# Gated mix of linear and softmax attention: 88 row-maximum units in the front instead of 76, in single PSUM banks

## The chip, the cores and the metric

The kernel runs on one core of one Trainium2 chip. The metric is device time in microseconds (us), the median of the runs of the whole kernel. Engines are called as in the profile: PE is TensorE (matmul), PEld its weight load, DVE VectorE, ACT ScalarE, POOL GpSimd, SP SyncE (here only a queue for DMA).

## The reference

Two attention layers work on the same `x` (2048 x 448, 16 heads of 28). A is linear attention with a learned feature map, B is full softmax attention. A gate per token mixes their projected outputs.

```python
g = _sigmoid((x * gate_w).sum(-1, keepdims=True))
a = _A_ref(x, A_wqkv, A_w_phi, A_wo)
b = _B_ref(x, B_wqkv, B_wo)
return g * a + (1 - g) * b

# A
pq = einsum("bhsd,hdf->bhsf", q, w_phi);  pk = einsum("bhsd,hdf->bhsf", k, w_phi)
phi_q = concatenate([softmax(pq), softmax(-pq)], -1);  phi_k = (the same of pk)
kv = einsum("bhsf,bhsd->bhfd", phi_k, v);  z = phi_k summed over s
o = einsum("bhqf,bhfd->bhqd", phi_q, kv) / (einsum("bhqf,bhf->bhq", phi_q, z) + 1e-6)

# B
p = softmax(einsum("bhqd,bhkd->bhqk", q, k) * Dh ** -0.5)
o = einsum("bhqk,bhkd->bhqd", p, v)
```

Each of `o` is then laid out as 2048 x 448 and multiplied by its `wo`.

## The kernel before

**Stages.** The sequences of PE, DVE, ACT and POOL are written out by hand: each engine does its instructions in the order of the Python code. The order of the DMA issues on SP is the framework's. PE never goes on past a matmul that waits, so the place of every piece of work in the code is its place on PE.

1. *Projections of B's queries and keys* (`proj_qk`, matrices `pqk`), stored through SP to a scratch tensor `qkd`. The first projections take tiles from a list `later`.
2. *The front loop*, `for i in range(2 * NT + 11)` (L711 on; NT = 16 tiles of 128 tokens). `t = i` is a key tile and `q = i - NT` a query tile. For t below 16 it projects the keys (`pk`) and values (`pva`) of A and makes their features on ACT, DVE and POOL; for q from 0 it does the queries (`pq`, `pft`, `pn`), the output projection of A (`poa`, stored as `gad`), and, from q = NT + 2, the value projection of B (`value_b`, `pvb`) for tiles 0 to 7. `tok_major` (L120) makes each projection as a run of eleven matmul passes over high and low parts of input and weights, and calls a given function ahead of each pass; weights are loaded by part, split and folded (`split_part`, `fold`) on DVE and ACT. `pace` and `tick` (L703, L705) count the passes of `pk` of a pair of key tiles and call `mx_unit` at given counts.
3. *The last loop of the front* (`for t in range(8, NT)`, L888): `value_b` for tiles 8 to 15, seven with `mx_unit` between passes (77 passes), the last one with the scores of step 0.
4. *The late loop*: 256 steps. A step is one block of 128 keys by 512 queries for each of four heads: four score matmuls (`st`, L856), four exponentials on ACT (`p`, L872), and four value matmuls (`pv`, L1000), which the trace records as eight. The output of a group of heads is normalized and stored to `od` (`finish`, f1 to f4), and read back for the output projection at the end.

**Row maxima.** The exponentials need the maximum of each row of B's scores ahead. They are made for 16 groups `gq` (four groups of heads by four blocks of queries), each as 16 units of four heads by a block of 128 queries by 512 keys; 256 units in all. Each unit has four matmuls of 28 rows in 32-row tiles (one for each head). NF = 76 units are made in the front by `mx_unit` (L259), the other 180 in the late loop by `mx_visit`. The names GM and QM are NF split into whole groups and blocks: 76 = 4 x 16 + 4 x 3.

In `mx_unit` the four matmuls lie two by two in tiles of two banks: `pmb` and then `pmd` (L286). The relu of the whole `pmd` (128 x 1024) on ACT follows at L289, then two DVE operations (L291) which add `pmb` to one half each and take the maximum into a column of `part`. The front gives `pmb` and `pmd` tiles of one tag `mx` with two buffers; behind the second change of pools (`ps_s_.close()`, L882) `mx` has two buffers and `md` one. `mx_visit` makes four matmuls `pm` (L323), one relu (L327), and three DVE operations (L332, L335).

**Order in the late loop.** Steps 1 to 104 go as *doubles*: two steps' scores, two steps' values, one visit. Steps 105 to 232 go as *singles*, each with a visit. Steps from 233 on are doubles without visits, with output projections `pob` between. So V visits over 232 steps leave 2 x (232 - V) steps in doubles, since each double saves one visit (`first`, L1126).

**Step 0.** `scores(0, ...)` makes the scores of its four heads in two-bank tiles, with one exponential (L864) for two heads. The eight banks of the late loop are then taken over one by one (L916), in an order that follows which of the front's banks come free first.

**Loads of the units.** `pair_load` and `pair_query` issue the loads of a unit's keys (`kp`) and queries (`qp`), and POOL converts them. `take_acts`, `take_exps`, `take_subs`, `take_lows`, and `take_diffs` run work that was put aside earlier.

Of the kernel before, what the change touches and what calls it, by code (L numbers as in the profile page):

```python
# [8 lines left out]
F32 = mybir.dt.float32  # L9
# [8 lines left out]
P = 128  # L18
# [10 lines left out]
NU = NG * NQ * 16  # L29
NF = 76  # L30
LOWEST = -3.0e38
LAST = 232
OUTS = (200, 238, 246, 206)
PROJ = (235, 243, 251)
# [7 lines left out]
def gated_mix_kernel(ctx, tc, xT, wqkB, wvB, wvA, wkAT, wqAT, phi, woA, woB,  # L42
# [17 lines left out]

    psn = [3, 2]

# [5 lines left out]

    def ps_mx(nm, d):
        return ps.tile([P, 2, 512], F32, tag="md" if d and psn[1] == 3 else "mx", name=nm,  # L70
                       bufs=1 if d and psn[1] == 3 else 2)

# [187 lines left out]
    def mx_unit():  # L260

        u = mxs["u"]
        if u == NF:
            return
        mx_fin()
        take_diffs(2)
        mxs["u"] = u + 1
        gq, r = divmod(u, 16)
        g, qb = divmod(gq, NQ)
        if gq < GM:  # L270
            c, qt = divmod(r, 4)
            hp, b = divmod(c, 2)
            col = 64 * gq + 16 * b + 4 * qt + 2 * hp
            if r in (4, 9):
                pair_query(gq + 1, r // 9)
        else:
            c, qt = divmod(r, QM)
            hp, b = divmod(c, 2)
            col = 64 * gq + 4 * QM * b + 4 * qt + 2 * hp
            if r == 0:  # L280
                mx_query(gq)
        qc, kc = mxs[("qp", gq, hp)], mxs[("kp", g, c)]
        pb, pd = ps_mx(f"pmb{u}", False), ps_mx(f"pmd{u}", True)
        for j in range(4):
            js = slice(32 * j, 32 * j + DH)
            nc.tensor.matmul((pb if j < 2 else pd)[:, j % 2, :], qc[js, qt * P:(qt + 1) * P],  # L286
                             kc[js, :], start=True, stop=True, tile_position=(32 * j, 0))
        rl = rlp.tile([P, 2, 512], F32, tag="rl", name=f"rl{u}", bufs=2 if psn[1] == 3 else 1)
        nc.scalar.activation(rl, pd, AF.Relu)  # L289
        for i in range(2):  # L290
            nc.vector.tensor_tensor_reduce(rl[:, i, :], pb[:, i, :], rl[:, i, :], 1.0, LOWEST,  # L291
                                           ALU.add, ALU.max, part[:, col + i:col + i + 1])
        if gq < GM and qt == 3 and qb == NQ - 1:
            pair_load(g + 1, c)
        if gq == GM and qt == QM - 1:
            mx_load(g, c)
        if r == 15:
            mx_reduce(gq)
# [312 lines left out]
    def first_units():  # L611
# [7 lines left out]
        pqs = [ps_s(f"pqk0_{m}") for m in range(3)] + [ps_pv("pqk0_3")]  # L619
        pr = [ps_mx(f"pqk_{i}", False) for i in range(2)]  # L620
        later.extend((pr[0][:, 0, :], pr[1][:, 0, :], pr[0][:, 1, :]))
        for _ in range(8):
# [29 lines left out]
    for n in range(4, NP):  # L652
# [19 lines left out]
        if n in (16, 18):  # L672
            split_part(wvA_s, "wvA", 450, (n - 16) // 2)
            take_lows()
        if n in (10, 12, 14, 17):
            fold(wkA_s, "k", {10: 0, 12: 1, 14: 2, 17: 3}[n])
        if n == 10:
# [34 lines left out]
    for i in range(2 * NT + 11):  # L712
# [4 lines left out]
        if t < NT and t % 2 == 0:  # L717
            mx_unit()
            passes = (55 if t < NT - 4 else 44) + (4 if t >= 4 else 0)
            pace["n"], pace["at"] = 4 if t >= 4 else 0, [k * passes // 4 for k in (1, 2, 3)]  # L720
        if q in (0, 1):
# [44 lines left out]
        take_subs()  # L766
        if t == 1:
            pair_load(0, 3)
# [33 lines left out]
        if NT + 3 <= q < NT + 10:  # L802
            mx_unit()
        if q == NT + 2:
            bd_s.close()
            vb = [value_tile(0)]
        if 0 <= q - NT - 2 < 8:
            value_b(q - NT - 2)
        if y >= 5 and y % 2 and tb - 2 < 8:
# [40 lines left out]
    def scores(s, i, js=range(4)):  # L850
# [8 lines left out]
        if s == 0:  # L859
            p = at.tile([P, 2, 512], F32, name=f"p{s}_{i}")  # L860
            st = ps_mx(f"st{s}_{i}", i)
            for jl in range(2):
                score(2 * i + jl, st[:, jl, :])
            nc.scalar.activation(p, st, AF.Exp, scale=SCALE)  # L864
            pts.setdefault(s, []).extend([p[:, 0, :], p[:, 1, :]])
            return
# [13 lines left out]
    load_nm(0)  # L880
    ps_s_.close()
    ps = ps_s_.enter_context(tc.tile_pool(name="psv", bufs=1, space=PSUM, reuse_waits="tile"))  # L882
    psn[:] = 2, 3
    rlp = fr_s.enter_context(tc.tile_pool(name="rlp", bufs=1, reuse_waits="tile"))
# [30 lines left out]

    for i in (3, 4, 1, 2, 5, 6, 0, None):  # L916
        if i is None:
            ps2.tile([P, 512], F32, tag="pv", name="pv_first", bufs=1)
        else:
            bank(i, f"first{i}")  # L920
# [116 lines left out]
    def finish(gq, s):  # L1037
# [14 lines left out]
        def f4():  # L1052
            st["o"], = normalize4(late_p, st["n"], f"b{gq}", 1)
            if g < NG - 1:
                for j in range(4):
                    r = (4 * g + j) * DH
                    nc.sync.dma_start(o_d[r:r + DH, :, qb * 512:(qb + 1) * 512],
                                      f32(st["o"][32 * j:32 * j + DH]))

# [6 lines left out]
        late.setdefault(s + 8, []).append(lambda: acts.append(f4))  # L1066
        if g == NG - 1:
            for tl in range(4):
# [183 lines left out]
```

## Time and profile before

| | us |
|---|---|
| median of the runs shown | 1016.2 (1015.07 to 1016.46) |
| the profiled execution | 1016.56 |
| its span | 1014.8 |
| PE busy | 1004.8 |
| ACT busy | 818.1 |
| DVE busy | 647.5 |
| POOL busy | 250.9 |
| front, to the start of the first double | 363.75 |
| doubles with a visit (52) | 230.53 |
| singles with a visit (128) | 330.72 |
| the rest, to the end | 89.80 |

The granted TensorE clock is full in all of the 40 slices of the page. The stretches of the last four lines are cut where the chain of waits changes its pattern. A row of that chain gives the start, its length, and the instructions that it is made of; a row of the timeline the start, the time of one or several instructions, engine, line, operation, output and input. A row of the groups has busy time, mean nanoseconds of one, and the idle time of the engine ahead of them with what ended it. PE counts as busy while a matmul waits in its pipeline, so its busy share alone does not tell a stretch that PE limits from one in which it waits.

### The profile page before, as it was taken

What the parts mean: (1) busy time and instruction counts of PE and PEld (TensorE: products, weight loads), DVE (VectorE), ACT (ScalarE), POOL (GpSimd) and SP (SyncE); (2) the same over time, 40 slices, a digit from 0 to 9 for tenths busy, and PEclk for the clock granted to TensorE, in tenths of its full rate; (3) what the DMA queues carried; (4) which work ended last, traced back from release to release, by engine and by line L of the source; (5) the groups of instructions that cost most, each with busy time, mean ns of one, the idle gap of its engine ahead of it and who ended that gap; (6) DMA issues with size and microseconds to landing.
All of it is one profiled execution on the core that took longest, in us unless ns stands there. A gap on an engine that the chain in (4) does not pass through costs nothing.

```text
span 1014.8 us, 17693 instructions
## 1 busy us (share of the span) xinstructions
PE 1004.8 (99%) x6344; PEld 566.7 (56%) x6344; DVE 647.5 (64%) x1335; ACT 818.1 (81%) x1534; POOL 250.9 (25%) x218
## 2 busy tenths in 40 slices
PE   8999999999999999999999999999999999999998
PEld 7777877777777754444444443333333333335665
DVE  5467767898765535445444568888888788885112
ACT  5355655577765699999999999999999999997662
POOL 1225435578734820220110120110110101100010
PEclk9999999999999999999999999999999999999999
DMA  8874010113233671223542233342232247310441
GB/s 294 289 250 120 33 52 31 43 37 95 84 97 98 153 164 38 58 66 74 112 96 72 71 90 81 79 105 56 73 85 61 71 98 200 96 38 30 136 145 55
DMA packets 64570, 99.62 MB, mean 98 GB/s; under 512 B 18134, under 2 KB 24902, under 8 KB 64482
## 3 DMA queue, kind: packets, MB, share of 16 engines
q1 hardware_dynamic: 64482, 98.49, 35.8%
q8 instruction: 50, 0.82, 0.4%
q14 instruction: 38, 0.31, 0.1%
HBM read 70.29 MB, written 27.78 MB: 97 GB/s over the span
## 4 chain that ended last, share of the span: by engine, by line
PE 95%; DVE 3%; ACT 1%; DMA 1%; issue 0%; POOL 0%; DVEq 0%; ACTq 0%; POOLq 0%
PE st L856 28%; PE pv L1000 24%; PE pm L323 8%; PE pqk L110 5%; PE poa L110 4%; PE pk L128 4%; PE pva L128 4%; PE pmb L286 3%; PE pob L110 3%; PE pq L110 2%; PE pvb L110 2%; PE pvb L128 2%; PE pn L538 1%; PE pqk L640 1%; PE pft L526 1%; DVE featq L453 1%
## 5 line engine op out<-in xcount | busy, mean ns | idle before, releaser
L872 ACT ACTIVATE p<-st 128x512 f32<-128x512 f32 x1020 | 525.1, 639 | 26.4 <-PE st L856 26.4
L335 DVE TENSOR_REDUCE part<-pm 128x1 f32<-128x512 f32 x405 | 258.8, 685 | 178.7 <-PE pm L323 178.7
L856 PE MATMUL st<-qst,kst 128*128 128x512 f32 x1024 | 299.5, 422 | 0.1
L1000 PE MATMUL pv<-p,vb 128*32 128x512 f32 x2048 | 259.7, 601 | 0.0
L856 PEld LDWEIGHTS st<-qst,kst 128*128 128x128 f32 x1024 | 171.0, 187 | 101.6 <-ACT p L872 39.3
L425 POOL TENSOR_TENSOR oUb<-oUb,rsb 128x512 f32<-128x512 f32 x15 | 19.3, 1289 | 492.4 <-DMA rsb<-rdb 360.1
L291 DVE CUSTOM_DVE_ANT_0 rl<-pmb,rl 128x512 f32<-128x512 f32 x152 | 98.3, 684 | 57.0 <-ACT rl L289 57.0
L327 ACT ACTIVATE rl<-pm 128x512 f32<-128x512 f32 x180 | 111.5, 620 | 10.4 <-PE pm L323 10.0
L323 PEld LDWEIGHTS pm<-kc,qc 28*128 28x128 f32 x720 | 34.4, 181 | 150.9 <-ACT p L872 102.3
L289 ACT ACTIVATE rl<-pmd 128x1024 f32<-128x1024 f32 x76 | 78.1, 1028 | 38.2 <-PE pmd L286 31.0
L1000 PEld LDWEIGHTS pv<-p,vb 128*32 128x32 f32 x2048 | 50.5, 108 | 96.0 <-issue 93.6
L332 DVE CUSTOM_DVE_ANT_0 rl<-pm,rl 128x512 f32<-128x512 f32 x135 | 92.0, 681 | 0.0
L323 PE MATMUL pm<-kc,qc 28*128 28x512 f32 x720 | 91.2, 495 | 0.0
L110 PE MATMUL pqk<-XH,wB 128*128 128x512 f32 x192 | 59.6, 397 | 1.7 <-DVE ev L578 1.7
L577 ACT CAST ev<-pqk 128x512 fp32r<-128x512 f32 x28 | 15.9, 588 | 36.7 <-PE pqk L110 32.0
L110 PE MATMUL poa<-woA_s,oTa 128*128 128x448 f32 x192 | 43.4, 375 | 0.0
L110 PEld LDWEIGHTS pqk<-XH,wB 128*128 128x128 f32 x192 | 35.3, 188 | 10.6 <-DVE ev L578 2.2
L1011 DVE SCALAR_TENSOR_TENSOR acc<-pob,gate,acc 128x448 f32<-128x448 f32 x12 | 8.2, 684 | 50.8 <-PE pob L110 50.8
L128 PE MATMUL pk<-wkA_s,XH 128*128 128x448 f32 x128 | 39.5, 382 | 0.0
L286 PE MATMUL pmd<-kp,qp 28*128 28x512 f32 x152 | 38.0, 496 | 0.8 <-DVE part L291 0.8
L110 PEld LDWEIGHTS poa<-woA_s,oTa 128*128 128x128 f32 x192 | 34.9, 188 | 6.2 <-issue 3.2
L128 PE MATMUL pva<-wvA_s,XH 128*128 128x450 f32 x128 | 37.8, 371 | 0.0
(155 smaller groups left out, 1196.1 us busy)
## 6 DMA issues: line engine op xcount, KB each, us to landing
qkd<-ev SPq DMA_DIRECT2D x28, 512.0 KB
qst<-qkd SPq DMA_DIRECT2D x64, 224.0 KB
kst<-qkd SPq DMA_DIRECT2D x64, 224.0 KB
od<-oTb SPq DMA_DIRECT2D x48, 112.0 KB
rsa<-rda SPq DMA_DIRECT2D x8, 512.0 KB
rsb<-rdb SPq DMA_DIRECT2D x15, 256.0 KB
gad<-ga SPq DMA_DIRECT2D x16, 224.0 KB
acc<-gad SPq DMA_DIRECT2D x4, 896.0 KB
```

What stands on the lines that cost most here:

```text
L110: nc.tensor.matmul(dst, l, r, start=i == 0, stop=i == len(todo) - 1)
L128: nc.tensor.matmul(dst[:, :n], l, r, start=i == 0, stop=i == len(todo) - 1, skip_group_check=True)
L286: nc.tensor.matmul((pb if j < 2 else pd)[:, j % 2, :], qc[js, qt * P:(qt + 1) * P], kc[js, :], start=True, stop=True, tile_position=(32 * ...
L289: nc.scalar.activation(rl, pd, AF.Relu)
L291: nc.vector.tensor_tensor_reduce(rl[:, i, :], pb[:, i, :], rl[:, i, :], 1.0, LOWEST, ALU.add, ALU.max, part[:, col + i:col + i + 1])
L323: nc.tensor.matmul(pm[j], mxs[("qc", gq)][js, qt * P:(qt + 1) * P], mxs[("kc", g, kb)][js, :], start=True, stop=True, tile_position=(32 * ...
L327: nc.scalar.activation(rl, pm[kb], AF.Relu if kb < 3 else AF.Copy)
L332: nc.vector.tensor_tensor_reduce(r, pm[j], r, 1.0, LOWEST, ALU.add, ALU.max, part[:, col + j:col + j + 1])
L335: nc.vector.tensor_reduce(part[:, col + j:col + j + 1], pm[j], AX.X, ALU.max)
L856: nc.tensor.matmul(st, kst_of[(g, kt // 4)][:, j, (kt % 4) * P:(kt % 4 + 1) * P], qst_of[gq][:, j, :], start=True, stop=True)
L872: nc.scalar.activation(p, sts[j], AF.Exp, scale=SCALE)
L1000: nc.tensor.matmul(pv[32 * j:32 * j + 32, :], vb[kt // 8][:, kt % 8, 4 * g + j, :], pt[j], start=kt == 0, stop=kt == NT - 1, tile_position ...
```

## The change

- NF goes from 76 to 88: twelve units more in the front (5 x 16 + 4 x 2), twelve visits fewer in the late loop (168). `first` becomes 128.
- A unit uses single banks: four tiles of tag `mx` with four buffers (six after the change of pools), in the order d0, d1, b0, b1. Two relus of 128 x 512, each followed by the DVE operation that reads it. The tile `rl` has two buffers of 512.
- `pace` asks for five units to a pair of key tiles for t below NT - 4 and four after.
- The change of pools moves from before the last loop to q = NT + 6 in the front loop. Behind it `s` has two banks and `mx` six.
- `value_b` of q = NT + 6 to NT + 9 has a unit behind its pass 4.
- The folds of the key weights go from n = 10, 12, 14, 17 to 11, 13, 15, 18; `pair_load(0, 3)` from t = 1 to t = 0.
- The three tiles `later` are single banks.
- A head's stores go from f4 at step s + 8 to f5 at s + 13; the fourth entry of OUTS, a step at which the output's data is read back, from 206 to 210.
- Step 0 makes one exponential for each head; the order of the first banks in the late loop follows the new tiles.

```diff
@@ -27,10 +27,10 @@
 SCALE = DH ** -0.5
 EPS = 1e-6
 NU = NG * NQ * 16
-NF = 76
+NF = 88
 LOWEST = -3.0e38
 LAST = 232
-OUTS = (200, 238, 246, 206)
+OUTS = (200, 238, 246, 210)
 PROJ = (235, 243, 251)
 
 
@@ -58,7 +58,7 @@
     ps = ps_s_.enter_context(tc.tile_pool(name="ps", bufs=1, space=PSUM, reuse_waits="tile"))
     dr = ctx.enter_context(tc.tile_pool(name="dr", bufs=1, space=DRAM))
 
-    psn = [3, 2]
+    psn = [3, 4, 2]
 
     def ps_s(nm):
         return ps.tile([P, 512], F32, tag="s", name=nm, bufs=psn[0])
@@ -66,9 +66,8 @@
     def ps_pv(nm):
         return ps.tile([P, 512], F32, tag="pv", name=nm, bufs=1)
 
-    def ps_mx(nm, d):
-        return ps.tile([P, 2, 512], F32, tag="md" if d and psn[1] == 3 else "mx", name=nm,
-                       bufs=1 if d and psn[1] == 3 else 2)
+    def ps_mx(nm):
+        return ps.tile([P, 512], F32, tag="mx", name=nm, bufs=psn[1])
 
 
     def scratch(nm, shape):
@@ -280,16 +279,18 @@
             if r == 0:
                 mx_query(gq)
         qc, kc = mxs[("qp", gq, hp)], mxs[("kp", g, c)]
-        pb, pd = ps_mx(f"pmb{u}", False), ps_mx(f"pmd{u}", True)
+
+        pm = [ps_mx(f"pm{'ddbb'[j]}{u}_{j % 2}") for j in range(4)]
         for j in range(4):
-            js = slice(32 * j, 32 * j + DH)
-            nc.tensor.matmul((pb if j < 2 else pd)[:, j % 2, :], qc[js, qt * P:(qt + 1) * P],
-                             kc[js, :], start=True, stop=True, tile_position=(32 * j, 0))
-        rl = rlp.tile([P, 2, 512], F32, tag="rl", name=f"rl{u}", bufs=2 if psn[1] == 3 else 1)
-        nc.scalar.activation(rl, pd, AF.Relu)
+            i = (j + 2) % 4
+            js = slice(32 * i, 32 * i + DH)
+            nc.tensor.matmul(pm[j], qc[js, qt * P:(qt + 1) * P], kc[js, :], start=True, stop=True,
+                             tile_position=(32 * i, 0))
         for i in range(2):
-            nc.vector.tensor_tensor_reduce(rl[:, i, :], pb[:, i, :], rl[:, i, :], 1.0, LOWEST,
-                                           ALU.add, ALU.max, part[:, col + i:col + i + 1])
+            rl = rlp.tile([P, 512], F32, tag="rl", name=f"rl{u}_{i}", bufs=psn[2])
+            nc.scalar.activation(rl, pm[i], AF.Relu)
+            nc.vector.tensor_tensor_reduce(rl, pm[2 + i], rl, 1.0, LOWEST, ALU.add, ALU.max,
+                                           part[:, col + i:col + i + 1])
         if gq < GM and qt == 3 and qb == NQ - 1:
             pair_load(g + 1, c)
         if gq == GM and qt == QM - 1:
@@ -617,8 +618,7 @@
             nc.sync.dma_start(raw[b][:, 1, :], xT[:, b, :512])
         x_loads(1)
         pqs = [ps_s(f"pqk0_{m}") for m in range(3)] + [ps_pv("pqk0_3")]
-        pr = [ps_mx(f"pqk_{i}", False) for i in range(2)]
-        later.extend((pr[0][:, 0, :], pr[1][:, 0, :], pr[0][:, 1, :]))
+        later.extend(ps_mx(f"pqk_{i}") for i in range(3))
         for _ in range(8):
             nc.tensor.matmul(pqs[3][:, :P], ident, ident, start=True, stop=True)
         for b in range(4):
@@ -672,8 +672,8 @@
         if n in (16, 18):
             split_part(wvA_s, "wvA", 450, (n - 16) // 2)
             take_lows()
-        if n in (10, 12, 14, 17):
-            fold(wkA_s, "k", {10: 0, 12: 1, 14: 2, 17: 3}[n])
+        if n in (11, 13, 15, 18):
+            fold(wkA_s, "k", {11: 0, 13: 1, 15: 2, 18: 3}[n])
         if n == 10:
             pair_query(0, 0)
             pair_load(0, 0)
@@ -716,8 +716,9 @@
         take_acts()
         if t < NT and t % 2 == 0:
             mx_unit()
-            passes = (55 if t < NT - 4 else 44) + (4 if t >= 4 else 0)
-            pace["n"], pace["at"] = 4 if t >= 4 else 0, [k * passes // 4 for k in (1, 2, 3)]
+            passes, n = (55, 5) if t < NT - 4 else (44, 4)
+            passes += 4 if t >= 4 else 0
+            pace["n"], pace["at"] = 4 if t >= 4 else 0, [k * passes // n for k in range(1, n)]
         if q in (0, 1):
             take_exps()
 
@@ -764,7 +765,7 @@
         if 2 <= q - 1 < NT:
             fq[q - 1] = features2(fq[q - 1], f"q{q - 1}")
         take_subs()
-        if t == 1:
+        if t == 0:
             pair_load(0, 3)
         if y >= 8 and y % 2 == 0 and tb - 4 < 8:
             num[tb - 4] = normalize3(*num[tb - 4], 2)
@@ -801,11 +802,15 @@
             turn(y - 2)
         if NT + 3 <= q < NT + 10:
             mx_unit()
+        if q == NT + 6:
+            ps_s_.close()
+            ps = ps_s_.enter_context(tc.tile_pool(name="psv", bufs=1, space=PSUM, reuse_waits="tile"))
+            psn[:2] = 2, 6
         if q == NT + 2:
             bd_s.close()
             vb = [value_tile(0)]
         if 0 <= q - NT - 2 < 8:
-            value_b(q - NT - 2)
+            value_b(q - NT - 2, lambda i: mx_unit() if i == 4 and q >= NT + 6 else None)
         if y >= 5 and y % 2 and tb - 2 < 8:
             num[tb - 2] = normalize2(ta, *num[tb - 2], f"a{tb - 2}", 2, True)
     ta_s.close()
@@ -857,12 +862,11 @@
                              qst_of[gq][:, j, :], start=True, stop=True)
 
         if s == 0:
-            p = at.tile([P, 2, 512], F32, name=f"p{s}_{i}")
-            st = ps_mx(f"st{s}_{i}", i)
-            for jl in range(2):
-                score(2 * i + jl, st[:, jl, :])
-            nc.scalar.activation(p, st, AF.Exp, scale=SCALE)
-            pts.setdefault(s, []).extend([p[:, 0, :], p[:, 1, :]])
+            for j in (2 * i, 2 * i + 1):
+                p, st = at.tile([P, 512], F32, name=f"p{s}_{j}"), ps_mx(f"st{s}_{j}")
+                score(j, st)
+                nc.scalar.activation(p, st, AF.Exp, scale=SCALE)
+                pts.setdefault(s, []).append(p)
             return
         sts = {j: bank(b, f"st{s}_{j}") for j, b in zip(js, i)}
         for j in js:
@@ -878,9 +882,6 @@
     stg = at
     load_q(0)
     load_nm(0)
-    ps_s_.close()
-    ps = ps_s_.enter_context(tc.tile_pool(name="psv", bufs=1, space=PSUM, reuse_waits="tile"))
-    psn[:] = 2, 3
     rlp = fr_s.enter_context(tc.tile_pool(name="rlp", bufs=1, reuse_waits="tile"))
     mx_unit()
     rest = NF - mxs["u"]
@@ -913,7 +914,7 @@
         return ps2.tile([P, 512], F32, tag=f"g{i}", name=nm, bufs=1)
 
 
-    for i in (3, 4, 1, 2, 5, 6, 0, None):
+    for i in (0, None, 2, 3, 1, 6, 5, 4):
         if i is None:
             ps2.tile([P, 512], F32, tag="pv", name="pv_first", bufs=1)
         else:
@@ -1051,11 +1052,12 @@
 
         def f4():
             st["o"], = normalize4(late_p, st["n"], f"b{gq}", 1)
-            if g < NG - 1:
-                for j in range(4):
-                    r = (4 * g + j) * DH
-                    nc.sync.dma_start(o_d[r:r + DH, :, qb * 512:(qb + 1) * 512],
-                                      f32(st["o"][32 * j:32 * j + DH]))
+
+        def f5():
+            for j in range(4):
+                r = (4 * g + j) * DH
+                nc.sync.dma_start(o_d[r:r + DH, :, qb * 512:(qb + 1) * 512],
+                                  f32(st["o"][32 * j:32 * j + DH]))
 
         if last:
             finish_last(gq)
@@ -1064,7 +1066,9 @@
         late.setdefault(s + 3, []).append(f2)
         late.setdefault(s + 7, []).append(f3)
         late.setdefault(s + 8, []).append(lambda: acts.append(f4))
-        if g == NG - 1:
+        if g < NG - 1:
+            late.setdefault(s + 13, []).append(f5)
+        else:
             for tl in range(4):
                 mids[PROJ[qb] + tl] = lambda tl=tl: project(qb, st["o"], tl)
 
```

## The prediction, written before the changed kernel was run

> **What bounds the kernel now.** I read the chain of waits of the page first, then the busy time by stretch with its boundaries at the changes of structure, then the chain inside each stretch.
>
> ```profile
> PE 95%; DVE 3%; ACT 1%; DMA 1%; issue 0%; POOL 0%; DVEq 0%; ACTq 0%; POOLq 0%
> ```
>
> TensorE ends 95% of the chain, but "busy TensorE" means two things, as the stretches show (us; busy time and count of PE, PEld, DVE, ACT, POOL; granted clock, DMA share, GB/s):
>
> ```profile
> 340.00:363.75 23.75, 23.70 (x124) 16.78 (x124) 13.85 (x44) 16.17 (x22) 21.30 (x13) 1.00 0.86 180
> 363.75:594.28 230.53, 230.53 (x1452) 105.52 (x1452) 109.41 (x222) 230.37 (x466) 25.62 (x26) 1.00 0.36 82
> 594.28:925.00 330.72, 330.72 (x2050) 126.90 (x2049) 270.41 (x544) 320.51 (x641) 31.80 (x29) 1.00 0.35 84
> ```
>
> The last loop of the front (first row) is a TensorE stretch: 23.70 of 23.75, ACT 16.17, DVE 13.85. 363.75 to 594.28 holds the 52 doubles (steps 1 to 104, one visit for two steps); 594.28 to 925.00 holds the 128 singles (a visit for each step). ACT is busy 230.37 of 230.53 in the doubles and 320.51 of 330.72 in the singles: there TensorE's time is waiting, and ACT sets the pace. 466 instructions in 230.53 are 0.495 us each, nine to a double (eight exponentials, one relu), which is also the distance of the starts below, although one lasts 0.6:
>
> ```profile
> 594.30 0.60 ACT L327 ACTIVATE rl<-pm 128x512 f32<-128x512 f32 x1
> 594.80 2.06 ACT L872 ACTIVATE p<-st 128x512 f32<-128x512 f32 x4
> ```
>
> The same stretches as the chain shows them, one double and then a single and the start of the next (start us, us, what):
>
> ```profile
> 367.03 2.17 PE st L856 x8
> 369.19 1.85 PE pv L1000 x16
> 371.05 0.44 PE pm L323 x4
> ...
> 596.89 1.40 PE st L856 x5
> 598.29 0.99 PE pv L1000 x8
> 599.29 0.43 PE pm L323 x2
> 599.72 0.90 PE st L856 x3
> 600.62 0.99 PE pv L1000 x8
> ```
>
> **The late loop gains 8.8.** Twelve more units in the front are twelve visits fewer, 168 for 180, so 24 steps go from singles to doubles (64 doubles, 104 singles). A double takes 230.53/52 = 4.433, 2.217 per step; a single 330.72/128 = 2.584. 24 x (2.584 - 2.217) = 8.8. The other end: if only the twelve relus went from a full ACT and the idle time of the singles stayed, 12 x 0.495 = 5.9. I take 8.8, since each mode keeps its rate over its whole stretch.
>
> **The front's price is 7.4.** A unit in the front and what it does to the run of projection passes it cuts:
>
> ```profile
> 247.37 2.46 PE poa L110 x12
> ...
> 308.20 0.42 PE pmb L286 x2
> 308.62 0.16 PE pmd L286 x2
> 308.78 2.65 PE poa L110 x12
> ...
> 338.32 1.63 PE pvb L128 x7
> 339.95 0.42 PE pmb L286 x2
> ```
>
> Twelve passes behind other passes take 2.46, 0.205 each; behind a unit 2.65, 0.19 more. Seven in the last loop: 7 x 0.205 = 1.44 against 1.63, again 0.19. So a unit costs its 0.42 to 0.43 and a restart of 0.19: 0.62. Each of the twelve new units cuts a run: in the built order four lie in the pairs of key tiles t = 4 to 10 (five units now), four within value tiles at q = 22 to 25, four in the last loop (15 units over its 77 passes, before 11). 12 x 0.62 = 7.4. Lower bound, where a restart falls on one that is there already: 12 x 0.43 = 5.2. I take 7.4. The fifth unit of pairs t = 0 and 2 can't come: its place is pass 44 and the two tiles count passes 0 to 43.
>
> **Waits that go: 2.7.** The row of 308.62 is one of seven between 295 and 333 in which the d matmuls wait about 0.16 for the bank that the unit before still reads: 1.1. Three more stand at t = 12 to 15, two of them shown:
>
> ```profile
> 168.59 0.50 PE pmd L286 x2
> ...
> 174.84 0.60 DVE rl L291
> ...
> 175.50 0.50 PE pmd L286 x2
> ...
> 182.13 0.49 PE pmd L286 x2
> ```
>
> Their d matmuls, which should add 0.01 after the b, add 0.49 to 0.50 each at 168.59 and 182.13, and at 175.50 the 0.50 ends a wait for the two reductions of the unit before. That is 0.48 for each of the outer two and about 0.6 for the middle one, 1.6 in all. With single banks a first half is free as soon as its own relu or reduction ends, and d needs only the unit before the last.
>
> **Waits that come: 3.6.** What a unit's banks wait for follows from these (ACT and DVE in the timeline; the unit starts at 317.55 and at 339.95):
>
> ```profile
> 317.66 0.63 ACT L553 ACTIVATE ga<-poa,gate 128x448 f32<-128x448 f32 x1 [1.57 <-PE poa L110]
> 318.19 1.02 ACT L289 ACTIVATE rl<-pmd 128x1024 f32<-128x1024 f32 x1
> ...
> 340.48 1.03 ACT L289 ACTIVATE rl<-pmd 128x1024 f32<-128x1024 f32 x1 [0.32 <-PE pmd L286]
> 341.55 0.69 DVE L291 CUSTOM_DVE_ANT_0 rl<-pmb,rl 128x512 f32<-128x512 f32 x1 [0.81 <-ACT rl L289]
> 342.17 0.08 DVE L291 DVE_READ_ACCUMULATOR2_ANT part<- 128x1 f32 x1
> ```
>
> The relu starts 0.53 behind the unit's start. Two half relus of 0.60 start 0.50 apart (the late rows), so the second ends at 0.53 + 0.50 + 0.60 = 1.63. With six banks in the order d0 d1 b0 b1, b0 and b1 of a unit take the banks of the relus of the unit just before; d0 and d1 those of the reductions two units before.
> - Last loop: 15 units in 77 passes, so 0.43 + 0.19 + 5.1 x 0.205 = 1.67 from unit to unit (2.06 now: 1.63 + 0.43). The second relu ends at 1.63, which leaves 0.04 for handing over the bank; I take that a unit is late by as much, 15 x 0.04 = 0.6.
> - q = 23 to 25: the unit within the value tile follows 0.43 + 0.19 + 4 x 0.205 = 1.44 after another whose relus stand behind the copy ga (317.66): the first relu starts at 318.19 - 317.55 = 0.64, the second ends at 1.74 and a handover later: 3 x 0.33 = 1.0.
> - The pools are now changed at q = 22: the unit behind the change takes its b banks from the reductions of the unit 1.44 before, done at 0.53 + 0.60 + 0.62 (distance of two reductions) + 0.69 + 0.08 = 2.5, with handovers 2.6: 1.2. The wait at the old place of the change (before the last loop) gives back 0.2.
> - Front: the unit behind the fold that moves to n = 18 finds DVE and ACT with the weights, and five units to a pair leave slack of 0 to 0.4 in the rest: 0.3 + 0.3, and about 0.4 of the 1.6 above stays at t = 12 to 15.
> Sum 0.6 + 1.0 + 1.2 - 0.2 + 0.6 + 0.4 = 3.6. From below: if none comes, 0; from above 3.6 + 3.9 (next part).
>
> **Moved at no cost.** The head's four stores go from step s + 8 to s + 13. They are issued on SP, behind no step of the chain (DMA has 1% of it in all); what would be late is the next use of the tile, 16 steps after the last, so 3 steps stand between. The first pair load comes one tile earlier; its conversion is POOL's, which has 0% of the chain, and the folds that move one pass on meet idle time of DVE in most tiles (if not hidden, the 0.3 above). The three `later` banks of the first projections end the sharing of a tile, for which one projection waits today:
>
> ```profile
> L110 PE MATMUL pqk<-XH,wB 128*128 128x512 f32 x192 | 59.6, 397 | 1.7 <-DVE ev L578 1.7
> ```
>
> The loads of the input set what follows, and they do not move, so I count 0 of this 1.7; it is the upper gain. In step 0 four exponentials of 512 stand for two of 1024: about 0.1 more, in the handover.
>
> **Sum.** -8.8 + 7.4 - 2.7 + 3.6 = -0.5, on the profiled execution's 1016.56 (span 1014.8 and 1.76 around it): 1016.1. It lies 0.36 above the median 1016.2, so 1015.7 against the median.
>
> **The rivals.**
> *Free rotation (faster).* The new short waits do not come: all 3.6 go, 1015.7 - 3.6 = 1012.1; half of them, 1013.9. For it: my latencies of 1.63 and 1.74 stand so close to the intervals that 0.05 decides. Against: in the present rows a d that waits for a unit's reductions does show its 0.16 seven times. The Trainium skill, Perfetto Trace Analysis, section on matmul optimizations, says that independent matmul groups should rotate through different banks so that the evacuation of one overlaps the next group's matmuls; six single banks do it more fully, and by that rule this rival is the one. The trace bears it out only where the interval is above the evacuation's length: at 2.06 in the last loop the row of ACT shows its 0.32 of idle time and no lateness.
>
> *The evacuation becomes the bound (slower).* In the last loop ACT and DVE, not TensorE, set the distance of units. Per unit ACT has two relus and 7/15 of a copy:
>
> ```profile
> L700 ACT COPY vb<-pvb 128x448 f32<-128x448 f32 x16 | 8.5, 530 | 12.2 <-PE pvb L110 9.4 <-POOL vb L693 1.7 <-PE pvb L128 0.9
> ```
>
> That is 0.50 + 0.60 + 0.25 = 1.35 of 1.67; DVE by the row of 340 to 363.75 has 13.85/11 = 1.26. Both fit on average, but the order is fixed by hand: a copy of 0.53 between a relu and its matmul moves the chain to about 1.97. Then 15 x 0.3 = 4.5 in place of 0.6, +3.9: 1015.7 + 3.9 = 1019.6. It decides from the point at which the second relu ends later than 1.67 behind its unit. Against: today the row of 340.48 shows ACT idle before each relu. The Trainium skill, TensorEngine Tiling (Array Packing), section on the PSUM bottleneck, says that tiling speeds up TensorE but not the evacuation, and advises vectorizing access over tiles in one bank; the change does the reverse, one relu of 1.03 becomes two of 0.60. By that rule this rival is what happens.
>
> *Late loads (slower).* The late loop's first key chunk now has less time between its last load and its first visit:
>
> ```profile
>   DMA kc<-qkd: 20.0, 1
>   POOL kc L197: 0.8, 1
> ```
>
> POOL waited 20.0 for it, and one visit waited 0.8 for POOL. Some 2 us of lead go, as the last loop starts its loads in proportion to its length; two visits at 1 to 1.5 each: +2.5, 1018.2.
>
> *It doesn't do what it says.* The five to two tiles do not come in two pairs, which the sum has. If the four others also failed, they would go to the last loop: 19 in 77 passes, 1.45 apart, each 0.2 late: +3.8, 1019.5.
>
> **Chances and range.** Forecast, a sum between 1014.2 and 1018.2: 0.42. Free rotation 0.29, evacuation 0.20, late loads 0.06, not as it says 0.03. A measurement of this kernel tells about 0.2%, 2.0 us, from no change (the three runs span 1.4): faster is below 1014.2, slower above 1018.2. Faster 0.29, same 0.42, slower 0.29. The range reaches from the full free rotation, 1012.1, to the evacuation's 1019.6: 1012.2 to 1019.6; the forecast's own is 1014.2 to 1018.2.
>
> **What would show it.** The doubles with visits should last 64 x 4.433 = 283.7 and the singles 104 x 2.584 = 268.7, 552.4 together for 561.25 now. The start of the doubles should move from 363.75 by +8.3. In the last loop units 1.67 to 1.70 apart agree, 1.9 or more is the evacuation. At q = 22 one wait of a b matmul for DVE near 1.2, none larger. The d matmuls at 295 to 333 should lose their 0.16. Wrong would be a wait for DMA at the first visits, singles slower than 2.6, or a front more than 10 longer.

## The result and the profile after

| | before | after |
|---|---|---|
| median of 7 runs, us | 1015.77 (1014.87 to 1016.46) | 1018.49 (1015.58 to 1020.85) |
| ratio to before, 95% interval | | 1.0023 (1.0013 to 1.0034) |
| profiled execution, us | 1016.56 | 1018.49 |
| its span, us | 1014.8 | 1016.7 |
| mean granted TensorE clock of the profiled execution | 1.000 | 0.998 |

The changed kernel is slower by 0.23%, some 2.3 us, where no measurable change was forecast (-0.5). The late loop did gain, the front lost more than that, and TensorE's clock was cut for 3.4 us near the start of the profiled run. Six of the seven runs have a mean granted clock of 0.997 or 0.998; the seventh, at 1.000, is the one of 1015.58.

First the page's share of the chain of waits after, to be held against the 95% of before:

```profile
PE 92%; DVE 4%; DMA 2%; ACT 1%; issue 0%; SPq 0%; DVEq 0%; ACTq 0%
```

TensorE's share fell by three points, but that is not 30 us of new waits: all waits in the view of TensorE's waits add up to 7.0 us, against 6.1 before. The chain is followed back through the wait near 33 us, and ahead of it now runs over the loads, stores and copies of the start, where before it ran mostly over TensorE; but for the waits below, TensorE was busy there in both. The view of TensorE's waits names those that differ most (waited for: us in total, times, longest), before and then after:

```profile
PE pqk L110 <- DVE ev L578: 1.7, 1, 1.7
PE pwk L393 <- issue: 1.4, 1, 1.4
```

```profile
PE pqk L109 <- DVE ev L579: 3.8, 1, 3.8
PE pv L1001 <- DVE oUb L405: 0.9, 1, 0.9
PE pmb L287 <- ACT rl L291: 0.7, 1, 0.7
```

The two waits of before near 22 and 36 us have become one of 3.8; two new ones stand in the late loop (pv) and among the first units (pmb). The stretches after (columns as in the prediction), around the wait of 3.8 and then the doubles, the singles and the end:

```profile
33.00:36.00 3.00, 0.04 (x1) 0.00 (x0) 0.65 (x1) 1.72 (x3) 0.60 (x1) 1.00 1.05 405
36.00:39.00 3.00, 2.18 (x5) 1.81 (x6) 1.93 (x4) 0.78 (x2) 2.00 (x9) 0.61 0.57 212
39.00:42.00 3.00, 3.00 (x16) 2.55 (x16) 0.23 (x1) 0.58 (x1) 0.00 (x0) 0.82 0.99 269
372.58:657.49 284.91, 284.91 (x1793) 130.98 (x1792) 134.94 (x274) 284.75 (x577) 33.35 (x33) 1.00 0.37 82
657.49:927.20 269.71, 268.79 (x1665) 103.19 (x1665) 219.89 (x442) 260.45 (x521) 24.15 (x22) 1.00 0.36 85
927.20:1016.70 89.50, 85.99 (x477) 55.35 (x476) 17.58 (x32) 48.18 (x95) 5.08 (x5) 1.00 0.31 101
```

TensorE does nothing from 33 to 36, and behind that the clock is 0.61 and 0.82 over three us each: (0.39 + 0.18) x 3 / 0.5 = 3.4 us at half clock, a loss of 1.7. A double takes 284.91/64 = 4.452, a single 269.71/104 = 2.593; both rates are those of before within 0.02, so each of the two modes works as it did (the seam between them comes below).

Where the time went shows when the same matmul is looked up in both traces (the n-th of its input and output, counted from 0), and 0.62 is taken off for each unit that one trace has ahead of it more. "Rest" is what is left, and grows where the changed kernel loses:

| matmul | before, us | after, us | units ahead | rest |
|---|---|---|---|---|
| projection of B, 112th of XH | 46.53 | 47.70 | 0 / 0 | +1.16 |
| first `pk` (key tile 0) | 67.46 | 69.57 | 5 / 5 | +2.11 |
| `pk` of key tile 12 | 160.12 | 165.62 | 29 / 33 | +3.02 |
| first `pq` behind the keys' end (41st) | 208.11 | 211.51 | 38 / 42 | +0.92 |
| `poa`, 108th | 296.47 | 299.65 | 52 / 56 | +0.70 |
| `pvb`, 59th (q = 24 to 25) | 331.19 | 338.56 | 63 / 71 | +2.41 |
| `pvb` at the end of the last loop | 357.34 | 367.27 | 75 / 87 | +2.50 |
| first `pv` of step 4 (late loop) | 373.58 | 383.51 | 76 / 88 | +2.49 |

From there on the difference itself: +9.71 at step 96, +2.18 at step 132, +2.24 at step 252. So the front grew by 12 x 0.62 = 7.44 and 2.5 of waits and half clock, and the late loop gave back 9.71 - 2.18 = 7.5 where the modes change, and 0.2 ahead of that.

### The profile page after: what moved, and what is told of

It is laid out like the page before. It is cut to its first block, busy times and chain, and to the rows that moved or that the text cites. A ratio compares the mean times of both kernels' runs of the same rounds, so it can differ in the third digit from the quotient of the medians.

```text
span 1016.7 us, 18066 instructions
## 1 busy us (share of the span) xinstructions
PE 1005.8 (99%) x6344; PEld 571.0 (56%) x6344; DVE 637.9 (63%) x1335; ACT 826.6 (81%) x1624; POOL 250.5 (25%) x218
## 4 chain that ended last, share of the span: by engine, by line
PE 92%; DVE 4%; DMA 2%; ACT 1%; issue 0%; SPq 0%; DVEq 0%; ACTq 0%
PE st L861 28%; PE pv L1001 24%; PE pm L324 7%; PE pqk L109 5%; PE pvb L127 4%; PE pk L127 4%; PE poa L109 4%; PE pva L127 4%; PE pmd L287 3%; PE pob L109 3%; PE pq L109 2%; DMA qkd<-ev 1%; PE pn L539 1%; PE pft L527 1%; PE pkv L482 1%; PE poL L1035 1%
## 5 line engine op out<-in xcount | busy, mean ns | idle before, releaser
L336 DVE TENSOR_REDUCE part<-pm 128x1 f32<-128x512 f32 x378 | 241.6, 686 | 197.6 <-PE pm L324 197.6
L292 DVE CUSTOM_DVE_ANT_0 rl<-pmb,rl 128x512 f32<-128x512 f32 x176 | 113.4, 682 | 43.6 <-ACT rl L291 43.1
L291 ACT ACTIVATE rl<-pmd 128x512 f32<-128x512 f32 x176 | 96.4, 601 | 34.9 <-PE pmb L287 28.2
L328 ACT ACTIVATE rl<-pm 128x512 f32<-128x512 f32 x168 | 103.6, 616 | 9.4 <-PE pm L324 8.0
L333 DVE CUSTOM_DVE_ANT_0 rl<-pm,rl 128x512 f32<-128x512 f32 x126 | 85.9, 682 | 0.0
L324 PE MATMUL pm<-kc,qc 28*128 28x512 f32 x672 | 85.0, 495 | 0.0
L287 PE MATMUL pmb<-kp,qp 28*128 28x512 f32 x176 | 48.2, 494 | 1.0 <-ACT rl L291 0.7
L287 PE MATMUL pmd<-kp,qp 28*128 28x512 f32 x176 | 44.4, 495 | 0.0
L127 PE MATMUL pvb<-wvB_s,XH 128*128 128x448 f32 x128 | 39.5, 384 | 0.0
```

The source lines that it names most:

```text
L127: nc.tensor.matmul(dst[:, :n], l, r, start=i == 0, stop=i == len(todo) - 1, skip_group_check=True)
L287: nc.tensor.matmul(pm[j], qc[js, qt * P:(qt + 1) * P], kc[js, :], start=True, stop=True, tile_position=(32 * i, 0))
L291: nc.scalar.activation(rl, pm[i], AF.Relu)
L292: nc.vector.tensor_tensor_reduce(rl, pm[2 + i], rl, 1.0, LOWEST, ALU.add, ALU.max, part[:, col + i:col + i + 1])
L324: nc.tensor.matmul(pm[j], mxs[("qc", gq)][js, qt * P:(qt + 1) * P], mxs[("kc", g, kb)][js, :], start=True, stop=True, tile_position=(32 * ...
L328: nc.scalar.activation(rl, pm[kb], AF.Relu if kb < 3 else AF.Copy)
```

## The experiments

All of them were run beside the kernel before on one chip for each group of four; ratios are to before. Spans and traces are of one execution each. The start of the kernel differs by up to 2.4 us from trace to trace with the time at which the input lands (the cast behind it starts between 32.60 and 35.04), so the place of a gain was read from the trace by the table's method, and the median was used for the sum.

**e1_warm: is the half clock the wait's doing?**

```diff
+        warm.append(ps_mx("warm"))
...
+        if n == 11:
+            for _ in range(14):
+                nc.tensor.matmul(warm[0][:, :P], ident, ident, start=True, stop=True)
         proj_qk(n, ev)
```

> The changed kernel with fourteen matmuls of the identity (about 0.21 us each, 3.0 in all) in front of the projection that waits 3.79 us near 33 us, into the fourth bank that is free there. Theory: TensorE's half clock of 3.41 us behind 36.68 us comes from TensorE having nothing to do for 3.8 us; with the filling it keeps full clock, and 1.7 us go: about 1016.8 in place of 1018.5. Rival: the half clock belongs to something else (the load of the input at that time, or chance): it stays, and the time stays within 0.5 us of the changed kernel's.

Median 1017.25, ratio 1.0012 (1.0003 to 1.0022). Ten of eleven runs had a mean clock of 0.999 or 1.000, against one of seven. The same stretch, with TensorE kept busy:

```profile
33.00:36.00 3.00, 3.00 (x29) 2.96 (x27) 0.68 (x1) 1.76 (x3) 0.64 (x1) 1.00 1.04 399
36.00:39.00 3.00, 2.37 (x12) 1.86 (x11) 1.89 (x4) 0.74 (x2) 1.97 (x9) 1.00 0.54 200
```

Full clock behind it. In the table's first row the rest is -0.42 in place of +1.16, 1.6 less: the theory's 1.7. The other rows' waits stayed.

**e2_copy: the wait where doubles turn into singles**

```diff
-        if n == 1 or mxs["f"] == len(flats):
+        if n == 1 or s == first + 1 or mxs["f"] == len(flats):
             take_copies()
```

> The changed kernel with the copies of a finished head taken ahead of the visit also in the last double (steps 127 and 128), as the singles do. Theory: the wait of the value matmuls for DVE's copy oUb at 658.7 us (0.92) goes, and with it ACT's 1.05 idle behind it: 1.0 us less than the changed kernel. Rival: the copy ahead delays the visit's reductions and their banks by as much, and the time stays.

Median 1018.03, ratio 1.0017 (1.0008 to 1.0026). In the changed kernel the chain at the transition is

```profile
655.19 1.85 PE pv L1001 x16
657.05 0.51 PE pm L324 x2
657.56 1.28 DVE part L336 x2
658.84 0.61 DVE oUb L405
659.45 0.14 issue
659.58 1.06 PE pv L1001 x8
660.65 0.43 PE pm L324 x2
661.08 1.42 PE st L861 x5
```

and with the copy first

```profile
656.84 1.85 PE pv L1001 x16
658.70 0.44 PE pm L324 x3
659.13 1.18 PE st L861 x4
660.31 1.00 PE pv L1001 x8
661.31 0.43 PE pm L324 x4
```

From the end of the last double's values to the end of the first single's, 657.05 to 660.65 is 3.60, and 658.70 to 661.31 is 2.61: 1.0 less, as expected. Over steps 96 to 132 the late loop gave back 8.59 in place of 7.53. The median doesn't show it: 1.0017 against 1.0023 for the changed kernel, with overlapping intervals. The start scatters by more; in the profiled run the wait at 33 us was 4.6, and half clock lasted twice as long. All twelve runs had a mean clock of 0.998 or less.

**e3_n11: eleven passes into the wait**

```diff
-        later.extend(ps_mx(f"pqk_{i}") for i in range(3))
+        later.extend(ps_mx(f"pqk_{i}") for i in range(4))
...
-        pq = later.pop(0) if later else ps_s(f"pqk{t}_{m}")
+        pq = later.pop(0) if later and n in (4, 5, 6, 11) else ps_s(f"pqk{t}_{m}")
```

> The changed kernel with projection n = 11 in the fourth single bank, free since the start, in place of a bank whose copy stands behind the cast of input that lands at 34 us. Theory: eleven passes (2.5 us) move into the wait of 3.79, which falls to about 1.3 to 2.0, too short for the half clock: 2.5 less of wait and 1.7 less of half clock, in all 3 to 4.2 us less than the changed kernel, near 1014.5. Rival: what follows waits for the same load in any case, so that only the half clock goes: 1.7.

Median 1016.47, ratio 1.0000 (0.9990 to 1.0009). At the table's first row the rest is -2.80, 4.0 less than in the changed kernel, the upper end of the expectation. At the first `pk` only 2.5 are left of it, since the first unit now waits for its keys (a new wait of 0.8 for POOL's kp). The median gained 2.3 (ratio 1.0023 to 1.0000), less than expected, and five of the eleven runs still had a mean clock of 0.998 or less. Even so, the whole loss of the change is gone with one projection that no longer waits for a copy behind the input's cast.

**e4_mid: the wait behind the change of pools**

```diff
-            value_b(q - NT - 2, lambda i: mx_unit() if i == 4 and q >= NT + 6 else None)
+            value_b(q - NT - 2, lambda i: mx_unit() if i == 4 and q >= NT + 7 else None)
```

> The changed kernel without the unit within the value tile of q = 22; the unit goes to the last loop, which then has 16 over its 77 passes. Theory: the wait of about 1.2 behind the change of pools goes, 16 units 1.61 apart in the last loop add 0.05 each at most: 0.4 to 1.2 us less. Rival: the next unit waits for the change of pools as long, or the last loop becomes paced by the relus: no difference or 0.5 to 1 us more.

Median 1018.07, ratio 1.0021 (1.0012 to 1.0030). In the changed kernel's chain the wait shows as

```profile
316.62 0.60 DVE rl L292
317.22 0.02 DVE part L292
317.24 0.04 issue
317.29 0.50 PE pmb L287
```

and it is absent here: between the 108th `poa` and the 59th `pvb` the rest grows by 0.24 in place of 1.71. The last loop with 16 units then adds 0.7 to 0.8 more than with 15, as the rival had it, so 0.6 to 0.8 remains. The median doesn't show it, a gain below what the start scatters (all eleven runs had a mean clock of 0.997 or 0.998).

**e5_fold17: the fold among the first units**

```diff
-        if n in (11, 13, 15, 18):
-            fold(wkA_s, "k", {11: 0, 13: 1, 15: 2, 18: 3}[n])
+        if n in (11, 13, 15, 17):
+            fold(wkA_s, "k", {11: 0, 13: 1, 15: 2, 17: 3}[n])
```

> The changed kernel with the last fold of the key weights back behind projection n = 17 (it had moved to 18). Theory: in the changed kernel the fold's copies on ACT and DVE meet the second part of a value weight, and the units of n = 18 and 19 and the one behind them lose 0.9 against before (by the places of the same matmuls in the two traces); back at 17 about half of that goes: 0.3 to 0.6 us less than the changed kernel, read in the trace between the projection passes at 53 and at 70 us. Rival: single banks and two relus alone make these units late, and nothing changes there.

Median 1018.51, ratio 1.0041 (1.0025 to 1.0058). A miss: between the projections and the first tiles of keys the rest still grows by 1.4 (from -1.36 to +0.04 at the ninth `pk`; in the changed kernel 1.16 to 2.3), and the wait of `pmb` for ACT is there with 0.7. The fold is not its cause.

**e13_split: the other neighbour of those units**

```diff
-        if n in (16, 18):
-            split_part(wvA_s, "wvA", 450, (n - 16) // 2)
+        if n in (17, 19):
+            split_part(wvA_s, "wvA", 450, (n - 17) // 2)
```

> The changed kernel with the two splits of A's value weights behind n = 17 and 19 in place of 16 and 18, and nothing else. Theory: the 1.0 to 1.3 that the units at n = 16 to 19 lose in the trace (the wait of 0.65 of a b matmul for ACT's relu among them) comes from the split between the relus; it falls to below 0.6. Rival: it comes from single banks, four to a unit, and stays.

Median 1018.46, ratio 1.0021 (1.0009 to 1.0033). The named wait of 0.7 is gone, but by the first `pva` the rest has grown by 0.9 (1.77 to 2.68) nevertheless. The split moved the loss by some units and did not remove it; that is nearer to the rival. What of it belongs to four single banks and what to the order of the copies stays open.

**e6_76: everything but the units**

```diff
-NF = 88
+NF = 76
```

> The changed kernel with NF = 76: single banks, the early change of pools, the folds and the stores as changed, but no unit more than before (three units left for the last loop, 104 steps of doubles). Theory: the twelve units move 7.4 us into the front and take about 7.5 out of the late loop (8.6 without the wait at step 128), so they are worth nothing, and what was lost was lost by the other edits: this kernel is as slow as the changed one, 1 to 2.5 us over before. Rival: the twelve units are what costs, and this kernel is as fast as before or faster by the waits that single banks take away, up to 2.7.

Median 1018.78, ratio 1.0023 (1.0012 to 1.0034), the same as the changed kernel. The twelve units are worth nothing within the interval; the loss belongs to the other edits. Its profiled execution is a lucky one (span 1013.8, wait of 2.1 at the start, full clock): four of its twelve runs had a mean clock of 0.999 or more, with a median of 1015.9, and the other eight 1019.8.

**e8_84, e10_84s, e12_88s, e14_76s: the waits taken out, with three numbers of units**

e8_84 has e3's edit and e4's, 84 units, and no unit at n = 16. e10_84s adds e13's splits. e12_88s is e10_84s with 88 units and e2's copies; e14_76s is e10_84s with 76.

```diff
-NF = 88
+NF = 84
...
-        if 16 <= n < 20:
+        if 17 <= n < 20:
             mx_unit()
```

> The changed kernel with 84 units, projection n = 11 in the fourth single bank, no unit at n = 16 and none within the value tile of q = 22. The doubles end with step 120, in the middle of a head. Theory: no long wait at 33 us and so no half clock, no wait for the change of pools, no wait for a head's copy where doubles turn into singles: 2.5 + 1.3 + 1.0 less than the changed kernel, 1013.5 to 1014.5, faster than both. Rival: the waits move on to the next load, and it ends within 1 us of before.

> As e8_84, with the two splits of A's value weights behind n = 17 and 19 in place of 16 and 18. In e8_84 the first split stands on ACT and DVE until its load lands at 54.46 us, the unit behind it waits 0.46 + 0.27 + 0.19, and TensorE runs 6.83 us at half clock. Theory: with the split behind the load these waits go, and with them the half clock there, 4 to 5.5 us of that profile and about 2 in the median: 1012.5 to 1013.5, faster than both kernels. Rival: the second split then comes late for the first values of A (pva), and the time moves there: as e8_84, 1015.

> As e10_84s with 88 units (17 in the last loop) and the copies of a head ahead of the visit in the last double. Theory: four more units are worth nothing where no wait comes with them (0.62 each against 0.72): within 0.7 us of e10_84s, rather above it since the last loop has a unit each 4.5 passes and its relus end behind the next unit's start (0.1 to 0.2 each). Rival: each unit kept out of the late loop still gains, 1 us or more below e10_84s.

> As e10_84s with 76 units (five left for the last loop, doubles to step 104). Theory: the units are worth little either way: within 1 us of e10_84s. By the prediction's prices, 8 units fewer are 5.0 less in the front and 5.8 more in the late loop, 0.8 us slower than e10_84s; a transition at step 104 and at step 120 cost the same. Rival: the units cost more in the front than they save, and this one is the fastest of all by 1 us or more.

| kernel | units | median, us | ratio to before |
|---|---|---|---|
| e8_84 | 84 | 1015.12 | 0.9992 (0.9983 to 1.0000) |
| e10_84s | 84 | 1011.75 | 0.9957 (0.9946 to 0.9969) |
| e12_88s | 88 | 1012.91 | 0.9966 (0.9954 to 0.9978) |
| e14_76s | 76 | 1012.45 | 0.9965 (0.9956 to 0.9975) |

e8_84 fell short (nine of its twelve runs had a mean clock of 0.998 or less), and the stretches of its trace say why (its second unit stands behind the split, whose load lands at 54.46):

```profile
54.50:58.00 3.50, 2.59 (x9) 1.12 (x7) 2.54 (x6) 3.11 (x6) 0.00 (x0) 0.99 1.05 393
58.00:61.00 3.00, 3.00 (x7) 2.08 (x8) 1.60 (x5) 0.47 (x1) 0.46 (x1) 0.50 0.40 125
61.00:64.00 3.00, 3.00 (x10) 2.42 (x9) 0.00 (x0) 0.23 (x1) 2.09 (x2) 0.50 0.85 317
```

Half clock again, without any long wait (the longest there is 0.46): a stretch in which TensorE was busy 2.59 of 3.50, for 1.57 of it with matmuls of 28 rows. With the split behind the load all of that goes, and in e10_84s two waits of TensorE are left in the view, neither of them from the change:

```profile
PE pqk L623 <- POOL ident masks.py:199: 1.4, 1, 1.4
PE pq L109 <- ACT oUa L405: 0.2, 1, 0.2
```

e10_84s is faster than both kernels, by 4.4 us than before. The medians are of 12, 6, 5 and 11 runs. The three numbers of units lie within 1.2 us of each other with overlapping intervals, and not in their order, so none of the three is shown to be the best.

**e9_before_n11: the same projection in the kernel before**

```diff
-        later.extend((pr[0][:, 0, :], pr[1][:, 0, :], pr[0][:, 1, :]))
+        later.extend((pr[0][:, 0, :], pr[1][:, 0, :], pr[0][:, 1, :], pr[1][:, 1, :]))
...
-        pq = later.pop(0) if later else ps_s(f"pqk{t}_{m}")
+        pq = later.pop(0) if later and n in (4, 5, 6, 11) else ps_s(f"pqk{t}_{m}")
...
-        if n in (10, 12, 14, 17):
-            fold(wkA_s, "k", {10: 0, 12: 1, 14: 2, 17: 3}[n])
+        if n in (11, 12, 14, 17):
+            fold(wkA_s, "k", {11: 0, 12: 1, 14: 2, 17: 3}[n])
```

> The kernel before with projection n = 11 in the fourth half of the two tiles that the first projections use, and the first fold behind n = 11 in place of 10. Theory: its two waits near 22 and 36 us (1.75 and 1.44) stay, but eleven passes come ahead of the second one: up to 1.4 us less than before, and fewer runs with half clock. Rival: the load of the input sets the time of n = 12 in any case, and nothing changes.

Median 1014.78, ratio 0.9995 (0.9986 to 1.0003): unclear in the sum. In its trace the wait of 1.4 is gone and the rest is -2.5 from 40 us on. That is more than expected, but 0.85 of it stands already behind the first wait, since this run's start was earlier; behind it 1.7 more are gained, in a run whose input landed early (cast at 32.60). Eight of its twelve runs had a mean clock of 0.999 or 1.000, 15 of the 29 of before beside it.

## Why the prediction was wrong

*What bounds the stretches* held. Doubles and singles kept their rates (284.91 and 269.71 for a forecast 283.7 and 268.7), and ACT set them: 284.75 of 284.91 busy in the doubles.

*The price of a unit in the front*, 0.62, held: with it the rests between two marks stay level wherever no wait is in between, and the last loop shows it (start, us, what):

```profile
361.92 0.42 PE pmd L287
362.35 0.01 PE pmb L287
362.35 1.21 PE pvb L127 x5
363.56 0.42 PE pmd L287 x2
```

Units are 1.64 apart, 0.43 + 1.21, and b adds 0.01 to 0.04. The 0.6 that I put on this loop did not come, and the rival of the evacuation, with its 1.9 or more, fell. So did free rotation, since the waits at q = 22 to 25 came, and the late loads: no visit waits for a load in the view of TensorE's waits.

*The late loop's gain of 8.8* was too large by 1.3. The size of a step was nearly right (by the starts of the value matmuls a step takes 2.226 from step 4 to 96 and 2.584 from 132 to 228, and 24 of them give 8.6), but I moved the end of the doubles from step 104 to 128 without asking what else happens there. 128 is 8 x 16, the last step of a head. In a double the copy of the finished sums (oUb) stands behind two reductions of the visit, and the next double covers that with eight scores; the first single has four. This is one of the two steps that failed: "each mode keeps its rate over its whole stretch" says nothing of the seam. e2_copy showed its price, 1.0 (with it the gain is 8.59).

*The start, counted at nothing*, is the other step that failed, and the one whose repair alone took the loss away (e3_n11). I saw that the single banks take away the wait of 1.75 and that the input's load sets what follows, and concluded that nothing changes ("I count 0 of this 1.7"). The load did hold the end of the stretch. But TensorE now reached it 2.7 earlier (33.04 for 35.72), and the waits of 1.75 and 1.44, with work between them, became one of 3.8. Of the 2.7, 2.0 is the first wait and its restart, gone with the single banks. The other 0.6 belongs to the run: the first matmuls of both traces start 0.43 apart and go over to 0.23, near 6 us after and 7.3 before. The cast of the input that ends the wait starts here, with what ACT had waited for; the copies on DVE follow, and then the matmul:

```profile
34.28 1.04 ACT L368 CAST XH<-xraw 128x1024 fp32r<-128x1024 f32 x1 [7.08 <-DMA xraw<-in_xT_dram]
...
35.35 0.69 DVE L376 TENSOR_TENSOR XH<-xraw,XH 64x512 fp32r<-64x512 f32 x1 [6.90 <-ACT XH L368]
36.08 1.89 DVE L579 TENSOR_TENSOR ev<-pqk,ev 128x512 fp32r<-128x512 f32 x3
...
36.82 1.22 PE L109 MATMUL pqk<-XH,wB 128*128 128x512 f32 x2 [3.79 <-DVE ev L579]
```

In all seven traces with this start (the changed kernel's, e1, e2, e4, e5, e6 and e13) the matmul goes on 2.54 behind the start of that cast, which lies between 33.10 and 35.04: the landing sets the end of the wait, and the wait left to TensorE was 2.1 to 4.6 (0.6 with e1's filling). Whether the change moves the landing itself can't be told from two traces with the start of before (34.55, and 32.60 in e9_before_n11).

Behind that wait came 3.4 us of half clock. e1_warm took it away by filling the wait, with everything else as it was, and e3_n11, in its trace, by giving the wait real work; both ends are shown. Of the start's +1.16, half clock is 1.6 by e1_warm. What is left against it is mostly that the cast started 0.27 earlier than in the trace of before; in e5_fold17 and e6_76, at full clock, the rest is -1.36 and -1.54 with casts 1.26 and 1.45 earlier, so that the single banks alone brought some 0.1. The Trainium skill, TensorE: Matmul & The Clock Gate, in its first part, says that the clock falls to half after at least one idle window of about 3.4 us, with windows that run freely; the trace agrees in the length of the cut (3.4 in the changed kernel) and in that 3.8 us of nothing to do suffice while 1.7 do not. It does not agree in e4_mid, where a wait of 3.1 by the profile, a little shorter than that window, sufficed. The prediction did not use the rule, which spoke against the change once the two waits are one.

*The waits that come at q = 22 to 25* were right: 1.2 was forecast for the change of pools, and the rest rises by 1.1 there (0.78 to 1.89); the three later ones show 0.36, 0.37 and 0.36 for a forecast 0.33. One that was not forecast, of 0.41, stands ahead of them at 308.77:

```profile
324.37 0.36 PE pmb L287 x2
...
331.31 0.37 PE pmb L287
...
338.26 0.36 PE pmb L287 x2
```

*The waits that go* went: the rest falls by 2.1 from key tile 12 to the first queries (1.2 net was forecast), and the d matmuls at 295 to 333 no longer wait.

*n = 16 to 19 and the pairs* were under-sized: 0.95 and 0.9 for a forecast 0.3 and 0.3. The fold, which I blamed ahead of time, was not the cause (e5_fold17), and neither was the place of the split alone (e13_split); what causes the loss there, and that of the pairs, stays open.

Added up against the forecast's terms: start +1.2, first units +0.65, pairs +0.6, late loop +1.3, and -0.9 at tiles 12 to 15. From the first queries to the end of the last loop the rest rose by 1.6 where the terms make 1.5, so that the 0.6 which the last loop did not cost went elsewhere, the wait of 0.41 among it: +0.1. Against this, 0.2 came back between steps 4 and 96, and 0.3 behind step 252. That is +2.4 over my sum of -0.5: +1.9, which is what the profiled spans differ by. That the twelve units themselves would be worth little (-8.8 + 7.4 = -1.4) was nearly right: the table has 7.4 against 7.7 given back, and e6_76 has the changed kernel's ratio without them.

## What to carry to other kernels

A wait that is taken away in front of a load need not vanish; here it joined the next one, and one idle stretch of TensorE of 3.8 us cost more than two of 1.75 and 1.44, because the clock was cut behind it. When the boundary between two modes of a loop is moved, look at what else falls on the new boundary. And where a change trades the same work between two places, work out the trade first: if it is near zero, the waits that come along are the whole result.

## What the runs showed of the hardware

The cut of TensorE's clock came in pieces of 3.4 us: one in the changed kernel, 6.8 in e2_copy behind a wait of 4.6, with the clock at 0.50 and 0.52 over its two stretches:

```profile
32.40:36.00 3.60, 0.34 (x2) 0.00 (x0) 0.15 (x1) 1.23 (x2) 0.10 (x1) 1.00 1.05 407
36.00:39.50 3.50, 2.18 (x5) 1.80 (x6) 2.43 (x4) 1.28 (x3) 2.50 (x9) 0.50 0.68 253
39.50:43.00 3.50, 3.50 (x12) 2.83 (x12) 0.00 (x0) 0.58 (x1) 0.00 (x0) 0.52 1.00 299
```

A wait of 3.1 (e4_mid) sufficed, one of 2.4 (e5_fold17) did not; one of 4.3 (e13_split) was followed by 3.4. In e2_copy the cut began at 36.02, inside the wait, and 1.3 us of its first piece were still wait; in e13_split 0.5. That this is why e2_copy had two pieces is a reading, not tried. In e8_84 the cut followed 3.5 us in which TensorE counted as busy for 2.59, the second half with matmuls of 28 rows only; that such matmuls count for less is a reading of one trace and was not tried. Also not expected: the kernel before had a mean clock of 0.998 or less in about half of its runs (18 of 35 beside the first four experiments) and was 1.0 us slower in them (1016.42 against 1015.40). One piece of 3.4 us at half clock is 0.5 x 3.4 / 1015 = 0.0017 of the mean, so that these runs have room for about one piece. That it stands at the same place there is likely but not shown, since the one trace of before has none.
